# A long convolution's kernel spectrum: kept on chip in data rows, with only a parts-exchanged copy moved

## The chip, the cores and the metric

One core of a Trainium2 chip. The metric is the device time of one execution in microseconds (us). Single executions of the kernel before lie between 512.5 and 520.0 us; one of 522.9 us was slow and is not used. The profile is of one execution each.

## The reference, cut to what matters

Two layers of local attention and two layers of a long convolution alternate. Both convolutions use the same filter `K`, so its spectrum is made once, in the first convolution, and used in both.

```python
def _B_ref(u, ...):                                   # called twice
    K  = einsum("dn,dnl,dn->dl", Cc, P, dB).real      # same K in both calls
    Kf = rfft(pad(K));  Uf = rfft(pad(u))
    y  = irfft(Uf * Kf)[..., :L]                      # + u * Dskip
```

## The kernel before: the parts that matter

The FFT is done with matrices. Per convolution there are two groups of channels (g = 0, 1), and per group 8 chunks of the spectrum. `f1` is the first step of the forward transform (evacuated into `a1s`), `f2` the second, `i1` and `i2` are the inverse. A PSUM tile is named `pb`; `evac` copies it out with ScalarE (ACT) or VectorE (DVE).

```python
def k_f2(self, g):                     # spectrum of the filter, first convolution only
    def consume(p2, ec):
        kf = self.wk.tile([P, DQG, EC], BF16, name="kf_sb")       # pool of 3
        self.evac(kf[:], p2[:]...)
        self.nc.sync.dma_start(self.kf_dram[g, ec]..., kf[:]...)  # 256 KB to HBM

def u_f2(self, g):                     # spectrum of u, and the products
    ...                                # kf_ring: 4 slots (8 in the second convolution)
    def consume(p2, ec):
        kc = ring[:, slot]
        for h in range(2):             # 2 x 256 KB from HBM
            nc.sync.dma_start(ring[h::2, slot], self.kf_dram[g, ec])
        ub = self.wk.tile([P, DQG, EC], BF16, name="ub")
        nc.scalar.copy(ub[:], p2[:]...)
        nc.vector.tensor_tensor(t1[...], ub[:], kc[:, 0], ALU.mult)
        nc.vector.tensor_tensor(t2[...], ub[:], kc[:, 1], ALU.mult)

def i1(self, g):
    z = self.z0 if g == 0 else ...     # z0 is the buffer xnT
    for t in range(NQT):
        p3 = self.ptile(...)
        for j in range(DQT):
            nc.tensor.matmul(p3[:, j], lhsT=t1[:, dql], rhs=wp_r,  start=True,  stop=False)
            nc.tensor.matmul(p3[:, j], lhsT=t2[:, dql], rhs=wpj_r, start=False, stop=True)
        self.evac(z[...], p3[...])     # with pattern act, act, act, dve: tiles 3 and 7 on VectorE

# main program, first convolution
zip_run(fb.f1(0, kp, "ka"))
zip_run(fb.f1(1, kp, "ka"), fb.k_f2(0), lead=2)
zip_run(fb.f1(0, u, "ua"), fb.k_f2(1), lead=2)
fb.pat = ("act", "act", "act", "dve")
zip_run(fb.f1(1, u, "ua"), fb.u_f2(0), lead=2)
zip_run(fb.u_f2(1), fb.i1(0), lead=4)          # products of group 1 beside inverse of group 0
fb.pat = ("act", "dve")
zip_run(fb.i1(1), fb.i2(0, None), lead=2)      # needs all products of group 1
```

Outside of sections marked with `manual_schedule`, the order of the instructions on each engine is chosen when the kernel is built, not by the order of these lines.

Of the kernel before, what the change touches and what calls it, by code (L numbers as in the profile page):

```python
# [11 lines left out]
ALU = mybir.AluOpType  # L12
# [3 lines left out]
BF16 = mybir.dt.bfloat16  # L16
# [3 lines left out]
P = 128  # L20
S = 2048
D = 512
# [3 lines left out]
NA = 16  # L26
NDT = 4
# [8 lines left out]
DQG = 64  # L36
EC = 16
NEC = 128 // EC
# [84 lines left out]
class LayerA:  # L123
# [88 lines left out]
            self.kT[:, ft, e0:e1, 1:P], self.kT[:, ft, e0 + 16:e1 + 16, 0:P - 1])  # L212

    def load_wv(self, pool):
        self.wv = pool.tile([P, NDT, D], BF16, name="wv")
        self.nc.sync.dma_start(self.wv[:], self.wsrc[:, :, 2 * D:3 * D])

    def load_wo(self, pool):
# [239 lines left out]
            u_apply(14, range(14, 16))  # L458

    def load_w2(self, w2_dram):  # L460
        w2 = self.keep.tile([P, P * P], BF16, name="w2_sb", tag="slot")
        self.w2 = w2[:].rearrange("p (e c) -> p e c", c=P)
        for c in range(4):
            self.nc.sync.dma_start(self.w2[:, c * 32:(c + 1) * 32, :], w2_dram[:, c * 32:(c + 1) * 32, :])

    def close_logits(self):
        self.lctx.close()
# [13 lines left out]
def build_b_consts(nc, cpool, tmp, w2_dram):  # L481
# [29 lines left out]
    def off_cols(name, rcol, v00, v10, v01, v11):  # L511
        o = tmp.tile([P, 2], F32, name=name)
        nc.vector.tensor_scalar(o[:, 0:1], rcol, float(v10 - v00), float(v00), ALU.mult, ALU.add)
        nc.vector.tensor_scalar(o[:, 1:2], rcol, float(v11 - v01), float(v01), ALU.mult, ALU.add)
        return o
# [2 lines left out]
    eo = tmp.tile([P, 1], F32, name="w2_eo")  # L518
    nc.vector.scalar_tensor_tensor(eo[:], ak, 64.0, d4k, ALU.mult, ALU.mult)
    nc.vector.tensor_tensor(off[:], off[:], eo[:].to_broadcast([P, 2]), ALU.add)  # L520
    wps = (("Wp", (4, 8, 0, 4)), ("WpJ", (8, 12, 4, 8)))
    wo = {name: off_cols("off_" + name, rim, *offs) for name, offs in wps}
    zt = tmp.tile([P, 1024], BF16, name="w2_zero")
    nc.gpsimd.memset(zt[:], 0.0)
# [82 lines left out]
class FftB:  # L607
# [58 lines left out]
            yield  # L666

    def k_f2(self, g):
        def consume(p2, ec):
            kf = self.wk.tile([P, DQG, EC], BF16, name="kf_sb")  # L670
            self.evac(kf[:], p2[:].rearrange("p e q -> p q e"))
            self.nc.sync.dma_start(self.kf_dram[g, ec].rearrange("p r q e -> (p r) (q e)"), kf[:].rearrange("p q e -> p (q e)"))
        yield from self.f2(g, "ka", consume)

    def u_f2(self, g):
        nc = self.nc
        if self.kf_ring is None:
            self.kf_ring = [self.ring_pool.tile([P, 4, 2, DQG, EC], BF16, name="kf_ring", tag="kp")]
            if self.ring2 is not None:
                self.kf_ring.append(self.ring2.tile([P, 4, 2, DQG, EC], BF16, name="kf_ring2"))  # L680
        t1 = self.gtile("t1", [P, DQG, P])
        t2 = self.gtile("t2", [P, DQG, P])
        self.S[g]["t"] = (t1, t2)

        def consume(p2, ec):
            ring, slot = self.kf_ring[self.nkf // 4 % len(self.kf_ring)], self.nkf % 4
            kc = ring[:, slot]
            self.nkf += 1
            for h in range(2):
                nc.sync.dma_start(ring[h::2, slot], self.kf_dram[g, ec])  # L690
            ub = self.wk.tile([P, DQG, EC], BF16, name="ub")
            nc.scalar.copy(ub[:], p2[:].rearrange("p e q -> p q e"))  # L692
            nc.vector.tensor_tensor(t1[:, :, ec * EC:(ec + 1) * EC], ub[:], kc[:, 0], ALU.mult)  # L693
            nc.vector.tensor_tensor(t2[:, :, ec * EC:(ec + 1) * EC], ub[:], kc[:, 1], ALU.mult)  # L694
        yield from self.f2(g, "ua", consume)

    def i1(self, g):
# [353 lines left out]
def kernel(  # L1051
# [16 lines left out]
    nc = tc.nc  # L1068
# [19 lines left out]
    la = LayerA(tc, nc, consts, lnst, A_wqkv, A_wo, 0, xnT, 2)  # L1088

    C = {}  # L1090
    with tc.manual_schedule(engines={ET.DVE, ET.Activation, ET.PE, ET.SP}):
        k_gen(tc, nc, consts["ident"], ins, kd, la, x_v, lnst, lambda sp: build_b_consts(nc, cpool, sp, w2_dram), C)
# [4 lines left out]
    kpp = krctx.enter_context(tc.tile_pool(name="kp", bufs=1))  # L1097
    kp = kpp.tile([P, P, NA, 4], BF16, name="k_perm", tag="kp")
# [38 lines left out]

    z0 = xnT[:].rearrange("p t c -> p (t c)").rearrange("p (m c) -> p m c", m=2 * NA)
    fb = FftB(tc, nc, C, consts["ident"], w2_dram, g2_dram, kf_dram, x_sb, 0)
    fb.z0, fb.ring_pool, fb.w2 = z0, kpp, la.w2  # L1140
    fb.open_mid()
    zip_run(fb.f1(0, kp, "ka"))
    zip_run(fb.f1(1, kp, "ka"), fb.k_f2(0), lead=2)
# [7 lines left out]
    la = LayerA(tc, nc, consts, lnst, A_wqkv, A_wo, 1, xnT, 1)  # L1151
# [19 lines left out]
    fb = FftB(tc, nc, C, consts["ident"], w2_dram, g2_dram, kf_dram, x_sb, 1)  # L1171
# [54 lines left out]
```

## Time and profile before

I cut the first convolution into three stages by VectorE's timeline: **K** from its first evacuation of `a1s` to the first product, **U** from the first to the last product, **I** from the end of the last product to the start of its last evacuation of `z`.

| kernel before | from, us | length, us | VectorE busy, us | TensorE clock |
|---|---|---|---|---|
| K: spectrum of the filter | 231.06 | 30.56 | 24.50 | 1.00 |
| U: spectrum of u, products, first inverse half | 261.62 | 31.79 | 23.53 | 0.93 |
| I: second inverse half | 293.41 | 14.98 | 6.12 | 0.82 |
| whole kernel | 0 | 511.9 | 414.7 | 0.94 |

These are lines of the windows view of the kernel before (from:to, length, then busy time and count of PE, PEld, DVE, ACT, POOL, then granted clock, DMA share, GB/s):

```profile
261.62:293.41 31.79, 20.21 (x406) 18.12 (x404) 23.53 (x36) 22.73 (x24) 0.35 (x1) 0.93 0.76 249
293.41:308.39 14.98, 14.94 (x173) 14.03 (x172) 6.12 (x5) 5.95 (x6) 0.00 (x0) 0.82 0.00 1
```

Stage I is TensorE's: busy 14.94 of 14.98 us. In U no engine is full. VectorE's timeline of the kernel before (start, length, instruction; in brackets the idle time before it and what ended it):

```profile
271.39 0.69 DVE L693 TENSOR_TENSOR t<-ub,kf_ring 128x1024 bf16<-128x1024 bf16 x1 [0.58 <-DMA kf_ring<-kf_dram]
...
275.10 0.69 DVE L693 TENSOR_TENSOR t<-ub,kf_ring 128x1024 bf16<-128x1024 bf16 x1 [0.70 <-DMA kf_ring<-kf_dram]
...
283.91 1.22 DVE L644 CAST xnT<-pb 128x1024 bf16<-128x1024 f32 x1 [4.93 <-PE pb L709]
...
288.58 1.22 DVE L644 CAST xnT<-pb 128x1024 bf16<-128x1024 f32 x1 [1.04 <-PE pb L709]
```

The short waits are for the ring, the long one is for an inverse tile: an `xnT` evacuation stands in VectorE's order before products that could have run.

### The profile page before, as it was taken

The page shows a single profiled execution, that of the slowest core. Times are in us where ns is not written, and L with a number is a line of the kernel's source. Part 1 is how long each engine was busy: PE and PEld are TensorE (multiplying, and loading weights), DVE is VectorE, ACT ScalarE, POOL GpSimd, SP SyncE. Part 2 cuts the span into 40 slices and gives each one's busy share as a digit, 9 for nine tenths or more (in the row PEclk, how much of TensorE's full clock was granted, in tenths as well). Part 3 has the DMA queues.
Part 4 walks back from the last instruction along what each step waited for, and adds up shares of the span by engine and source line. Part 5 has one row for each costly group of instructions (what it writes and reads, how often), then busy time and mean ns, then how long its engine had stood idle before and what let it go on. Part 6 is the DMA issues. An engine that isn't in the chain of part 4 may idle for free.

```text
span 511.9 us, 12810 instructions
## 1 busy us (share of the span) xinstructions
PE 379.2 (74%) x5528; PEld 283.9 (55%) x5528; DVE 414.7 (81%) x580; ACT 336.5 (66%) x538; POOL 35.1 (7%) x38
## 2 busy tenths in 40 slices
PE   1000428898998998888876596889998898877795
PEld 1000216665655776667765495445657676676694
DVE  7799979999899999959776647728999999659843
ACT  5999597755554688588696534574543466679832
POOL 2000120000000011210000000100000022200000
PEclk9999978999998799899998989799997899979989
DMA  8803500111128338221788502540041061206314
GB/s 223 341 1 38 85 0 3 42 24 45 19 71 261 109 97 333 72 83 71 257 264 305 181 1 70 178 164 2 2 122 25 1 272 58 79 7 193 139 44 123
DMA packets 56122, 56.40 MB, mean 110 GB/s; under 512 B 28573, under 2 KB 45570, under 8 KB 54786
## 3 DMA queue, kind: packets, MB, share of 16 engines
q1 hardware_dynamic: 55922, 55.46, 34.8%
q8 instruction: 43, 0.70, 0.6%
q10 hardware_dynamic: 144, 0.13, 0.2%
q14 instruction: 13, 0.11, 0.1%
HBM read 38.67 MB, written 13.24 MB: 101 GB/s over the span
## 4 chain that ended last, share of the span: by engine, by line
PE 41%; DVE 23%; ACT 20%; DMA 6%; issue 4%; SPq 2%; POOL 2%; DVEq 0%; POOLq 0%; ACTq 0%
DVE pav L343 6%; PE pp L202 6%; PE pq L296 5%; PE po L351 4%; PE pq L143 4%; PE pk L975 3%; PE L L254 3%; DVE prod L247 3%; PE pb L708 3%; PE pb L709 2%; ACT ub L692 2%; DMA kf_dram<-kf_sb 2%; POOL ln_rstd L101 2%; ACT xnT L195 2%; PE pq L363 2%
## 5 line engine op out<-in xcount | busy, mean ns | idle before, releaser
L351 PE MATMUL po<-ident,pav 128*128 128x128 bf16 x1024 | 68.3, 229 | 14.4 <-DVE pav L343 14.4
L351 PEld LDWEIGHTS <-pav 128*128 128x128 bf16 x1024 | 63.8, 103 | 22.8 <-DVE pav L343 19.2
L343 DVE TENSOR_TENSOR pav<-attn,v_ext 128x4096 bf16<-128x4096 bf16 x32 | 72.9, 2283 | 0.8 <-PE po L351 0.8
L247 DVE TENSOR_TENSOR prod<-qT,kT_ext 128x4096 bf16<-128x4096 bf16 x29 | 65.8, 2285 | 3.2 <-PE L L254 3.1
L101 POOL TENSOR_TENSOR ln_rstd<-ln_rstd,ln_mh 128x4 f32<-128x4 f32 (+1 forms) x18 | 29.4, 1634 | 291.2 <-DVE ln_rstd L100 245.2
L708 PE MATMUL pb<-Wp,t 128*128 128x128 bf16 x256 | 36.0, 237 | 12.1 <-DVE t L693 7.4
L202 PE MATMUL pp<-xnT,kT_ext 128*128 128x512 bf16 x128 | 34.4, 416 | 7.2 <-ACT xnT L195 6.9
L644 ACT CAST a1s<-pb 128x1024 bf16<-128x1024 f32 x34 | 34.1, 1029 | 7.7 <-PE pb L655 6.8
L354 ACT CAST oT<-po 128x512 bf16<-128x512 f32 x32 | 18.5, 579 | 30.9 <-PE po L351 30.9
L193 PE MATMUL pt<-ident,x_blk 128*128 128x128 bf16 x64 | 5.6, 241 | 41.5 <-ACT x_blk L118 41.5
L709 PE MATMUL pb<-WpJ,t 128*128 128x128 bf16 x256 | 35.2, 237 | 0.4 <-DVE t L694 0.4
L664 PE MATMUL pb<-a1s,w_sb 128*128 128x64 bf16 x768 | 29.6, 194 | 7.9 <-ACT ub L692 4.2
L363 PE MATMUL pq<-wop,oT 128*128 128x512 bf16 x128 | 34.9, 397 | 0.0
L975 PE MATMUL pk<-B_t,A_t 128*64 128x84 bf16 (+1 forms) x512 | 25.3, 210 | 12.3 <-issue 9.3
L692 ACT CAST ub<-pb 128x1024 bf16<-128x1024 f32 x32 | 32.1, 1058 | 2.9 <-DVE t L694 2.9
L664 PEld LDWEIGHTS <-w_sb 128*128 128x128 bf16 x768 | 26.6, 98 | 11.2 <-issue 8.8
L708 PEld LDWEIGHTS <-t 128*128 128x128 bf16 x256 | 27.1, 107 | 9.4 <-DVE t L693 9.3
L298 ACT CAST v_ext<-pq 128x512 bf16<-128x512 f32 x32 | 18.8, 586 | 20.4 <-PE pq L296 20.4
L254 PEld LDWEIGHTS <-prod 128*128 128x128 bf16 x928 | 27.4, 96 | 8.0 <-DVE prod L247 1.6
L975 PEld LDWEIGHTS <-A_t 128*64 128x64 bf16 (+1 forms) x512 | 23.1, 110 | 15.6 <-issue 12.4
L296 PE MATMUL pq<-wv,xnT 128*128 128x512 bf16 x128 | 30.4, 379 | 0.0
L143 PE MATMUL pq<-xnT,kT_ext 128*128 128x512 bf16 x128 | 30.4, 380 | 0.0
(204 smaller groups left out, 883.3 us busy)
## 6 DMA issues: line engine op xcount, KB each, us to landing
kf_ring<-kf_dram SPq DMA_DIRECT2D x64, 256.0 KB
w_sb<-w_dram SPq DMA_DIRECT2D x8, 1024.0 KB
w_dram<-w_zero SPq DMA_DIRECT2D x1, 4096.0 KB
kf_dram<-kf_sb SPq DMA_DIRECT2D x16, 256.0 KB
v_ext<-v_ext SPq DMA_DIRECT2D x4, 784.0 KB
x_blk<-in_A_x_dram SPq DMA_DIRECT2D x4, 512.0 KB
kT_ext<-in_A_wqkv_dram SPq DMA_DIRECT2D x4, 512.0 KB
x_sb<-in_A_x_dram SPq DMA_DIRECT2D x4, 512.0 KB
```

Source lines behind the costliest of these rows:

```text
L143: nc.tensor.matmul(pq[:], lhsT=self.wqk[:, dt, ft * P:(ft + 1) * P], rhs=self.xnT[:, dt, q * 512:(q + 1) * 512], start=(dt == 0), stop=(dt ...
L202: nc.tensor.matmul(pp[:], lhsT=self.wqk[:, dt, D + ft * P: D + (ft + 1) * P], rhs=self.xnT[:, dt, b * 512:(b + 1) * 512], start=(dt == 0), ...
L247: nc.vector.tensor_tensor(pr, self.qT[q][:, ft].unsqueeze(1).to_broadcast([P, W, 4, P]), kap, ALU.mult)
L254: self.nc.tensor.matmul(L[:, al, w, ft * 8:(ft + 1) * 8], lhsT=pr[:, w, al, :], rhs=self.c["ind8"][:], start=False, stop=True, skip_group_ ...
L296: nc.tensor.matmul(pp[:], lhsT=xnT[:, dt, a * P:(a + 1) * P], rhs=wv[:, dt, :], start=(dt == 0), stop=(dt == NDT - 1))
L343: nc.vector.tensor_tensor(pv[:], attn[:, n % 4].unsqueeze(2).to_broadcast([P, W, DH, H]), vap, ALU.mult)
L351: nc.tensor.matmul(po[:, ft, :], lhsT=pvf[:, w, ft * P:(ft + 1) * P], rhs=ident[:], start=(w == 0 and ft == 0), stop=(w == W - 1), skip_gr ...
L363: nc.tensor.matmul(pw[:], lhsT=oT[:, ftp, :], rhs=wo[:, ftp, :], start=False, stop=(ftp == NDT - 1))
L664: nc.tensor.matmul(p2[:, j, :], lhsT=self.w2[:, ec * EC + j, :], rhs=a1s[:, ec * EC + j, :], start=True, stop=True)
L708: nc.tensor.matmul(p3[:, j, :], lhsT=t1[:, dql, :], rhs=wp_r, start=True, stop=False)
L709: nc.tensor.matmul(p3[:, j, :], lhsT=t2[:, dql, :], rhs=wpj_r, start=False, stop=True)
L975: nc.tensor.matmul(o, lhsT=lhs, rhs=Bt[:, ri, c * CH + ql].rearrange("p b g -> p (b g)"), start=(not half and j % 4 == 0 and ri == 0), sto ...
```

## The change

The intent: in the first convolution the filter spectrum need not go to HBM and back. Its 16 chunks get 16 places of their own in SBUF, whose old contents are dead by then, and `t1 = U*K` reads them in place. Only the copy with exchanged real and imaginary rows, for `t2`, is moved, from SBUF to SBUF. Since the rows of `t1` and `t2` now stand for other parts, the inverse tables get other offsets. The store to HBM stays, for the second convolution, which reloads in three transfers a chunk instead of two.

```diff
     def load_wv(self, pool):
-        self.wv = pool.tile([P, NDT, D], BF16, name="wv")
+        self.wv_pool = pool
+        self.wv = pool.tile([P, NDT, D], BF16, name="wv", tag="wv")
 ...
+    def spare(self):
+        rest = [self.w2_rest] + [self.keep.tile([P, 2 * DQG * EC], BF16, name=f"kn_{i}", tag="qT", bufs=2)[:] for i in range(2)]
+        rest.append(self.wv_pool.tile([P, 2 * DQG * EC], BF16, name="kn_2", tag="wv")[:])
+        ...                                      # cut into 9 places
 ...
-    wps = (("Wp", (4, 8, 0, 4)), ("WpJ", (8, 12, 4, 8)))
+    wps = (("Wp", (4, 12, 0, 8)), ("WpJ", (8, 8, 4, 4)))
 ...
     def k_f2(self, g):
+        if g == 0:
+            self.nat = list(self.spare)
+        else:
+            kp2 = self.ring_pool.tile([P, 8, DQG, EC], BF16, name="kf_nat", tag="kp")
+            self.kf_ring = kp2
+            self.nat += [kp2[:, 4 + i] for i in range(4)]
         def consume(p2, ec):
-            kf = self.wk.tile([P, DQG, EC], BF16, name="kf_sb")
-            self.evac(kf[:], p2[:].rearrange("p e q -> p q e"))
+            n = g * NEC + ec
+            if n >= len(self.nat):
+                self.nat.append(self.wk.tile([P, DQG, EC], BF16, name="kf_sb")[:])
+            kf = self.nat[n]
+            self.evac(kf, p2[:].rearrange("p e q -> p q e"))
             ...                                  # store to kf_dram as before
+    def kf_pair(self, g, ec):
+        n, sync = self.nkf, self.nc.sync
+        self.nkf += 1
+        if self.tag == 0:
+            kn, ks = self.nat[n], self.kf_ring[:, n % 4]
+            for h in range(2):
+                sync.dma_start(ks[h::2], kn[1 - h::2])        # 2 x 128 KB inside SBUF
+            return kn, ks
+        ...                                      # second convolution
+        sync.dma_start(kc[0::2], self.kf_dram[g, ec])
+        for r in range(2):
+            sync.dma_start(kc[1::2, r], self.kf_dram[g, ec, :, 1 - r])
+        return kc[:, 0], kc[:, 1]
 ...
-            nc.vector.tensor_tensor(t1[...], ub[:], kc[:, 0], ALU.mult)
-            nc.vector.tensor_tensor(t2[...], ub[:], kc[:, 1], ALU.mult)
+            nc.vector.tensor_tensor(t1[...], ub[:], kn, ALU.mult)
+            nc.vector.tensor_tensor(t2[...], ub[:], ks, ALU.mult)
```

More of the change, by code (lines that the diff above doesn't have):

```diff
@@ L460, in load_w2 @@
     def load_w2(self, w2_dram):
-        w2 = self.keep.tile([P, P * P], BF16, name="w2_sb", tag="slot")
-        self.w2 = w2[:].rearrange("p (e c) -> p e c", c=P)
+        w2 = self.keep.tile([P, NDT * (2 * D + (NA + 14) * P)], BF16, name="w2_sb", tag="slot")
+        self.w2 = w2[:, 0:P * P].rearrange("p (e c) -> p e c", c=P)
+        self.w2_rest = w2[:, P * P:]
         for c in range(4):
             self.nc.sync.dma_start(self.w2[:, c * 32:(c + 1) * 32, :], w2_dram[:, c * 32:(c + 1) * 32, :])
+    def spare(self):
+        rest = [self.w2_rest] + [self.keep.tile([P, 2 * DQG * EC], BF16, name=f"kn_{i}", tag="qT", bufs=2)[:] for i in range(2)]
+        rest.append(self.wv_pool.tile([P, 2 * DQG * EC], BF16, name="kn_2", tag="wv")[:])
+        n = DQG * EC
+        return [r[:, i * n:(i + 1) * n].rearrange("p (q e) -> p q e", e=EC) for r in rest for i in range(r.shape[-1] // n)]
     def close_logits(self):
@@ L668, in k_f2 @@
     def k_f2(self, g):
-        def consume(p2, ec):
-            kf = self.wk.tile([P, DQG, EC], BF16, name="kf_sb")
-            self.evac(kf[:], p2[:].rearrange("p e q -> p q e"))
-            self.nc.sync.dma_start(self.kf_dram[g, ec].rearrange("p r q e -> (p r) (q e)"), kf[:].rearrange("p q e -> p (q e)"))
-        yield from self.f2(g, "ka", consume)
+        if g == 0:
[4 more added lines that the diff above has]
+            self.nat += [kp2[:, 4 + i] for i in range(4)]
+        def consume(p2, ec):
+            n = g * NEC + ec
[3 more added lines that the diff above has]
+            self.evac(kf, p2[:].rearrange("p e q -> p q e"))
+            self.nc.sync.dma_start(self.kf_dram[g, ec].rearrange("p r q e -> (p r) (q e)"), kf.rearrange("p q e -> p (q e)"))
+        yield from self.f2(g, "ka", consume)
+    def kf_pair(self, g, ec):
[6 more added lines that the diff above has]
+            return kn, ks
+        if self.kf_ring is None:
+            self.kf_ring = [pool.tile([P, 4, 2, DQG, EC], BF16, name=f"kf_ring{i}")
+                            for i, pool in enumerate((self.ring_pool, self.ring2))]
+        kc = self.kf_ring[n // 4 % 2][:, n % 4]
+        sync.dma_start(kc[0::2], self.kf_dram[g, ec])
+        for r in range(2):
+            sync.dma_start(kc[1::2, r], self.kf_dram[g, ec, :, 1 - r])
+        return kc[:, 0], kc[:, 1]
     def u_f2(self, g):
         nc = self.nc
-        if self.kf_ring is None:
-            self.kf_ring = [self.ring_pool.tile([P, 4, 2, DQG, EC], BF16, name="kf_ring", tag="kp")]
-            if self.ring2 is not None:
-                self.kf_ring.append(self.ring2.tile([P, 4, 2, DQG, EC], BF16, name="kf_ring2"))
         t1 = self.gtile("t1", [P, DQG, P])
@@ L685, in consume @@
         def consume(p2, ec):
-            ring, slot = self.kf_ring[self.nkf // 4 % len(self.kf_ring)], self.nkf % 4
-            kc = ring[:, slot]
-            self.nkf += 1
-            for h in range(2):
-                nc.sync.dma_start(ring[h::2, slot], self.kf_dram[g, ec])
+            kn, ks = self.kf_pair(g, ec)
             ub = self.wk.tile([P, DQG, EC], BF16, name="ub")
             nc.scalar.copy(ub[:], p2[:].rearrange("p e q -> p q e"))
-            nc.vector.tensor_tensor(t1[:, :, ec * EC:(ec + 1) * EC], ub[:], kc[:, 0], ALU.mult)
-            nc.vector.tensor_tensor(t2[:, :, ec * EC:(ec + 1) * EC], ub[:], kc[:, 1], ALU.mult)
+            nc.vector.tensor_tensor(t1[:, :, ec * EC:(ec + 1) * EC], ub[:], kn, ALU.mult)
+            nc.vector.tensor_tensor(t2[:, :, ec * EC:(ec + 1) * EC], ub[:], ks, ALU.mult)
         yield from self.f2(g, "ua", consume)
@@ L1139 @@
     fb = FftB(tc, nc, C, consts["ident"], w2_dram, g2_dram, kf_dram, x_sb, 0)
-    fb.z0, fb.ring_pool, fb.w2 = z0, kpp, la.w2
+    fb.z0, fb.ring_pool, fb.w2, fb.spare = z0, kpp, la.w2, la.spare()
     fb.open_mid()
```

## The prediction

> **What bounds the kernel now.** I read the page first, then the chain of waits and VectorE's timeline in the stretch that the diff touches, then the windows view. The whole-kernel shares do not decide anything: no engine is full, and the chain passes from one to the other.
>
> ```profile
> PE 379.2 (74%) x5528; PEld 283.9 (55%) x5528; DVE 414.7 (81%) x580; ACT 336.5 (66%) x538; POOL 35.1 (7%) x38
> ...
> PE 41%; DVE 23%; ACT 20%; DMA 6%; issue 4%; SPq 2%; POOL 2%; DVEq 0%; POOLq 0%; ACTq 0%
> ```
>
> The reader should see that transfers hold only 6% of the chain, some 30 us; a change of transfers can win a part of that and no more. Which part is in the chain by time:
>
> ```profile
> 237.10 1.14 DVE kf_sb L644
> 238.26 2.43 DMA kf_dram<-kf_sb
> ...
> 243.19 3.94 DMA kf_dram<-kf_sb
> ...
> 248.48 3.49 DMA kf_dram<-kf_sb
> ...
> 253.34 2.41 DMA kf_dram<-kf_sb
> ...
> 268.94 4.05 DMA kf_ring<-kf_dram
> ```
>
> Four stores of the kernel spectrum and one reload, 16.3 us, lie on the chain. The reason is buffers: the spectrum leaves PSUM into a pool of three (kf_sb), so evacuation n waits until store n-3 has landed. VectorE's timeline shows it (in brackets: idle before, and its releaser):
>
> ```profile
> 240.81 3.49 DVE L644 CAST kf_sb<-pb 128x1024 bf16<-128x1024 f32 x3 [0.32 <-DMA kf_dram<-kf_sb]
> 245.03 1.23 DVE L644 CAST a1s<-pb 128x1024 bf16<-128x1024 f32 x1 [0.73 <-PE pb L655]
> 247.23 3.48 DVE L644 CAST kf_sb<-pb 128x1024 bf16<-128x1024 f32 x3 [0.98 <-DMA kf_dram<-kf_sb]
> 252.09 3.49 DVE L644 CAST kf_sb<-pb 128x1024 bf16<-128x1024 f32 x3 [1.38 <-PE pb L664]
> 255.88 1.22 DVE L644 CAST kf_sb<-pb 128x1024 bf16<-128x1024 f32 x1 [0.30 <-DMA kf_dram<-kf_sb]
> 259.20 1.23 DVE L644 CAST kf_sb<-pb 128x1024 bf16<-128x1024 f32 x1 [2.10 <-DMA kf_dram<-kf_sb]
> ```
>
> Groups of three evacuations and then a pause: the signature of a pool of three. The windows view (length, busy time of each engine, clock, DMA share, GB/s) gives the two stages, and the same second stage in the second convolution:
>
> ```profile
> 231.00:260.60 29.60, 23.48 (x661) 21.21 (x661) 23.54 (x22) 22.77 (x25) 0.00 (x0) 1.00 0.56 188
> 260.60:293.50 32.90, 21.32 (x437) 19.03 (x435) 24.55 (x36) 23.75 (x26) 0.35 (x1) 0.93 0.76 250
> 461.00:487.30 26.30, 18.65 (x413) 16.87 (x407) 23.34 (x36) 22.93 (x25) 0.00 (x0) 0.99 0.49 162
> ```
>
> In the first line VectorE is busy 23.5 of 29.6 us. The second line (first convolution, products of spectra) and the third (second convolution) hold the same 32 products, but the first one takes 6.6 us more, with DMA engines at 0.76 against 0.49. The third line needs no reload for the first half: the ring was filled long before. So it is a picture of the stage without transfers in its way.
>
> [...] the stores here took 2.41 to 3.94 us[...] windows of 2 us after the stall of 270 to 273.7 show a clock of 0.76 and 0.50. [...] the products here take 0.60 us for 1024 elements start to start against 1.16 us for an evacuation[...].
>
> **The change, part by part.**
>
> (1) First convolution, making the spectrum. The 16 chunks get 16 places of their own (3 in the rest of the weight slot, 4 in two q tiles, 2 in the wv tile, 4 in the ring, 3 kf_sb). The compiled order shows the evacuations waiting on TensorE alone; the 16 stores stay, for the second convolution, but nobody waits for them. Before: from 231.06 to 260.48, 29.4 us, VectorE does 5 + 14 + 1 = 20 evacuations of 1.16 us (3.48 for three) = 23.2 us; 6.0 us are idle: 3.7 put down to stores, 2.3 to TensorE. The last is partly an echo: ScalarE, too, waited 1.75 us for a store at 244.6, which held a PSUM buffer. TensorE comes close behind, one pair of tiles each 1.14 us (236.58 to 237.72 to 238.86), so I leave 1.0 us of bubbles: 24.3 us. Gain 5.1 us.
>
> (2) First convolution, products. Before: per chunk two transfers of 256 KB from HBM, 16 x 0.52 = 8.4 MB, after a store landed. Now: one copy with exchanged parts, two transfers of 128 KB inside SBUF, 4.2 MB; t1 reads the spectrum in place. The ring of swapped copies still has four slots. At the pace of the second convolution (a chunk each 1.2 us), from the second product of chunk n-4 to that of chunk n there are 1.2 x 4 - 0.6 = 4.2 us. The copy needs two issues at about 0.5 us (median 0.587 for the old ones)[...] VectorE idled 0.58, 0.42 and 0.70 us. VectorE from first to last product: before 261.62 to 293.41 = 31.8 us; second convolution 461.50 to 487.27 = 25.8 us. The 6.0 us between split into about 2 us of waits on the ring and about 4 us in which VectorE waited for TensorE (4.93 and 1.04 against 2.11), partly at half clock after the stall. I count 4.9 us, leaving 1.1 for copies that come late and for the other order of the inverse tiles.
>
> (3) Second convolution: reload in three transfers instead of two per chunk, same 8.4 MB, 16 more issues at 0.6 us = 9.6 us of the queue. The first eight chunks are loaded in the attention before. For the last eight, 3 x 0.6 = 1.8 us a chunk from 462.8 on: chunk 8 is there at about 467, needed at 473.0; chunk 15 at about 480, needed at 486.0. Cost 0.
>
> (4) The inverse tables: other numbers in the same instructions, cost 0. The count of matmuls and products stays.
>
> Sum: 5.1 + 4.9 = 10.0 us, all in front of the rest of the kernel, so it passes to the end: 516.4 - 10.0 = 506.4 us, a ratio of 0.981.
>
> **Rivals.**
> A. The stage of products keeps its length. The swapped copies are still a chain of release, issue, landing and product over four slots; if landing takes 4 us under the remaining stores[...], the chain is 0.1 + 1.0 + 4.0 + 0.6 = 5.7 us for four chunks, 1.4 instead of 1.2 each, and the scheduler puts more products ahead of the inverse evacuations (14 chunks before the first one, where it was 11), so a wait there holds TensorE too. [...] Against it: half the bytes. Then only (1) and some 2 us stay: 509.5 us.
> B. TensorE becomes the bound. With no stalls it runs at 1.14 us a pair against VectorE's 1.16; a clock below 1 there would give back 1 to 3 us. Against it: it had 1.00 all through that stage. About 508.5 us.
> C. More than the stalls goes away: without idle gaps the clock stays up in the inverse transform too (it was 0.58 from 293.5 to 300, 0.75 in the same place of the second convolution). Another 2 us: 504 us.
> D. The evacuation was hidden and only the order changes: 515 us. The idle times on the chain speak against it.
>
> **Range and chances.** The sum and rivals span 504 to 509.5; repeated runs of the kernel before spread from 514.65 to 519.14, which adds some 2 us. Range 502 to 512. The 2% line is at 506.0, just under my number: rival C and the full 6.0 us of part 2 lie beyond it, A and B on this side. Faster 0.47, same 0.52, slower 0.01.
>
> **What would show it.** Step 1 right: no evacuation of the spectrum waits for a store, and the 20 evacuations span about 24.3 us. Step 2 right: products from first to last in about 27 us, waits for the swapped copies under 1 us in sum; wrong (rival A) if VectorE waits for them again and again. Step 3 right: the second convolution's products still take about 25.8 us with no wait on the ring. Rival B: a clock under 1 in the first stage. Rival C: the inverse transform after the last product shorter than its 18 us. The prediction fails upwards if part 2 gains nothing, downwards if the clock gains as well.

## The result, and the profile after

| | median, us | range, us | ratio to before, 95% interval |
|---|---|---|---|
| before, 4 runs | 515.55 | 514.65 to 519.14 | |
| changed, 4 runs | 499.58 | 497.57 to 500.10 | 0.9671 [0.9615, 0.9726] |
| changed, second time, 6 runs (before: 516.28) | 501.20 | 500.61 to 502.02 | 0.9717 [0.9679, 0.9756] |

All outputs are right. Executions over 1.5% slower than the fastest of the same kernel are left out of the means. Here and below a ratio is the mean time of one kernel's runs over that of the other's of the same rounds, so it is not quite the ratio of the medians beside it. The change is faster by some 3%, and the number predicted, 506.4 us, was too high by 6.8 us; the measured median lies 2.4 us under the range (0.8 us under it the second time).

The same three stages, from the profiled executions:

| stage | before, us | after, us | gain, us | predicted gain, us |
|---|---|---|---|---|
| K | 30.56 | 25.82 | 4.74 | 5.1 |
| U | 31.79 | 24.15 | 7.64 | 4.9 |
| I | 14.98 | 11.94 | 3.04 | 0 |
| start of K | 231.06 | 231.65 | -0.59 | 0 |
| after the last `z` of I to the end | 203.51 | 204.74 | -1.23 | 0 |
| span | 511.9 | 498.3 | 13.6 | 10.0 |

(The profiled execution of before was a quick one, 513.64 us, and that of after the slowest of its four; so the two spans differ by 13.6 us where the medians differ by 16.0.)

The windows view of the changed kernel, same cuts:

```profile
257.47:281.62 24.15, 18.73 (x408) 17.02 (x407) 23.11 (x35) 22.43 (x24) 0.35 (x1) 1.00 0.53 181
281.62:293.56 11.94, 11.90 (x170) 11.19 (x168) 6.12 (x6) 5.95 (x6) 0.00 (x0) 1.00 0.01 4
```

VectorE does the same 23 us of work in U, now in 24.15 us instead of 31.79: of 8.26 us of idle time 1.04 are left. Stage I holds the same work for TensorE, at a clock of 1.00 instead of 0.82. VectorE's timeline of the changed kernel answers to the groups of three evacuations that the prediction shows, and to the waits above:

```profile
237.60 3.47 DVE L653 CAST w_sb<-pb 128x1024 bf16<-128x1024 f32 x3
241.00 4.60 DVE L653 CAST kn<-pb 128x1024 bf16<-128x1024 f32 x4
...
247.78 4.60 DVE L653 CAST kf_nat<-pb 128x1024 bf16<-128x1024 f32 x4
...
276.86 1.21 DVE L653 CAST xnT<-pb 128x1024 bf16<-128x1024 f32 x1
...
279.80 1.23 DVE L653 CAST xnT<-pb 128x1024 bf16<-128x1024 f32 x1
```

No bracket on any of them: no evacuation of the spectrum waits for a store, and no inverse tile is waited for. The experiments below show that transfers alone do not explain the second. Counting VectorE's multiplications around the two `xnT` evacuations gives **22, 4 and 6 in the kernel before, 28, 3 and 1 in the changed one**. The diff doesn't order this: the build chose another order. In the chain of waits of the changed kernel transfers have gone from 6% to 2%:

```profile
PE 42%; DVE 25%; ACT 21%; issue 5%; DMA 2%; SPq 2%; POOL 2%; POOLq 0%; DVEq 0%; ACTq 0%
```

Why is stage I shorter? In the kernel before the last six multiplications come after the second `xnT` evacuation, and TensorE has nothing to do meanwhile. Its timeline, and the clock in windows of 2 us (third number from the end of a line):

```profile
292.86 0.50 PE L708 MATMUL pb<-Wp,t 128*128 128x128 bf16 x3 [4.32 <-DVE t L693]
...
293.76 0.31 PE L708 MATMUL pb<-Wp,t 128*128 128x128 bf16 x1
293.87 0.31 PE L709 MATMUL pb<-WpJ,t 128*128 128x128 bf16 x1
```

```profile
289.00:291.00 2.00, 0.00 (x0) 0.00 (x0) 2.00 (x4) 1.18 (x2) 0.00 (x0) 1.00 0.96 305
...
293.00:295.00 2.00, 2.00 (x19) 1.74 (x18) 0.41 (x1) 0.00 (x0) 0.00 (x0) 0.50 0.01 4
...
297.00:299.00 2.00, 2.00 (x18) 1.81 (x17) 1.11 (x1) 0.52 (x1) 0.00 (x0) 0.51 0.00 0
```

After 4.32 us without work the clock is at 0.50, and matmuls start each 0.11 us (293.55 to 298.13) instead of each 0.055 us (before the wait, 286.0 to 286.9). The clock is back at 1.00 at 298.96, 6.1 us after the first of them. In the changed kernel only one multiplication is left there, and TensorE's waits at that place are 0.69 and 0.30 us:

```profile
280.56 0.22 PE L737 MATMUL pb<-Wp,t 128*128 128x128 bf16 x1 [0.69 <-ACT xnT L653]
...
281.08 0.27 PE L751 MATMUL pb<-x_sb,ident 128*128 128x256 bf16 x1 [0.30 <-DVE xnT L653]
```

So the theory after the result: (a) the evacuation gains what was worked out; (b) in U the change acts twice, by fewer bytes to wait for and by the order of VectorE's instructions, which also takes away the 4.32 us of idle time, after which the clock in I was at 0.50. A rival for (b): the order is beside the point, and the gain in U is that of the transfers' source (SBUF instead of HBM) or size. The experiments take these apart.

### The profile page after: what moved, and what is told of

The parts are those of the page before. It is cut to its first block, busy times and chain, and to the rows that moved or that the text cites.

```text
span 498.3 us, 12784 instructions
## 1 busy us (share of the span) xinstructions
PE 372.0 (75%) x5492; PEld 280.7 (56%) x5528; DVE 414.1 (83%) x580; ACT 336.0 (67%) x538; POOL 34.9 (7%) x38
## 4 chain that ended last, share of the span: by engine, by line
PE 42%; DVE 25%; ACT 21%; issue 5%; DMA 2%; SPq 2%; POOL 2%; POOLq 0%; DVEq 0%; ACTq 0%
DVE pav L344 7%; PE pp L202 6%; PE po L352 5%; PE pq L297 4%; PE pq L143 4%; PE pk L1004 3%; DVE prod L248 3%; PE L L255 3%; ACT ub L721 3%; PE pb L664 3%; PE pb L738 2%; ACT xnT L195 2%; PE pb L737 2%; ACT a1s L653 2%; PE pq L364 2%
## 5 line engine op out<-in xcount | busy, mean ns | idle before, releaser
L202 PE MATMUL pp<-xnT,kT_ext 128*128 128x512 bf16 x123 | 33.1, 408 | 7.6 <-ACT xnT L195 6.9
L737 PE MATMUL pb<-Wp,t 128*128 128x128 bf16 x256 | 32.5, 224 | 7.0 <-DVE t L722 3.1
L364 PE MATMUL pq<-wop,oT 128*128 128x512 bf16 x112 | 31.4, 395 | 1.4 <-ACT oT L355 0.4
L738 PE MATMUL pb<-WpJ,t 128*128 128x128 bf16 x256 | 32.0, 225 | 0.0
L205 ACT CAST kT_ext<-pp 128x512 bf16<-128x512 f32 x32 | 18.4, 586 | 15.2 <-PE pp L202 15.2
```

The lines of the kernel that those rows point to most:

```text
L202: nc.tensor.matmul(pp[:], lhsT=self.wqk[:, dt, D + ft * P: D + (ft + 1) * P], rhs=self.xnT[:, dt, b * 512:(b + 1) * 512], start=(dt == 0), ...
L737: nc.tensor.matmul(p3[:, j, :], lhsT=t1[:, dql, :], rhs=wp_r, start=True, stop=False)
```

## The experiments

**One part alone: places for the spectrum.** The kernel before, with the evacuation spread over nine places used in turn; reload and order as before.

```diff
-            kf = self.wk.tile([P, DQG, EC], BF16, name="kf_sb")
+            kf = self.spare[(g * NEC + ec) % len(self.spare)]
```

> Part 1 alone: the kernel before, with nine places of their own for the evacuated spectrum in turn (so evacuation n waits for store n-9, not n-3), and the full reload of 512 KB a chunk kept. VectorE's compiled order is that of the kernel before. Theory (the two parts add): from VectorE's first evacuation to the first product 25.8 us instead of 30.6, the products from first to last still about 31.8 us, the clock still near 0.5 in the inverse transform after them; 5 us won, about 510.5 us. Rival (the transfers only pile up behind the faster evacuations, and the reloads now wait for the stores): the products stretch by 2 to 4 us, and only 1 to 3 us are won, 512.5 to 514.5 us.

Measured: 510.49 us, ratio 0.9902 [0.9864, 0.9939], that is 5.1 us (1 - 0.9902 of some 515.8). K is 27.05 us; U gets no shorter, 33.35 us. VectorE's timeline in U, of this kernel:

```profile
269.93 0.69 DVE L702 TENSOR_TENSOR t<-ub,kf_ring 128x1024 bf16<-128x1024 bf16 x1 [1.32 <-DMA kf_ring<-kf_dram]
...
282.57 1.23 DVE L653 CAST xnT<-pb 128x1024 bf16<-128x1024 f32 x1 [4.58 <-PE pb L718]
```

Part 1 holds, in size too. The ring's waits and the long wait for the inverse tile are all still there, so nothing of the gain in U comes from part 1. (In the profiled run K is 3.51 us shorter, I is 1.01 shorter and U 1.56 longer, 2.96 us in all; the ratio's interval stands for 3.1 to 7.0 us, so that 5.1 meets the forecast to a tenth is luck.) K comes in two lengths, 25.8 and 27.0 us, also in later kernels that do not differ from each other there, and the clock tells them apart: in the four runs with 27.0 us TensorE ran at half clock for 3.41 us near the start of K, in those with 25.8 us nowhere in K. This run had the longer one (windows view):

```profile
234.03:237.44 3.41, 3.41 (x72) 3.41 (x68) 2.45 (x2) 2.43 (x3) 0.00 (x0) 0.50 0.02 5
```

**Where the swapped copy comes from.** The changed kernel, but each copy is read from the stored spectrum in HBM; same size, same number.

```diff
-                sync.dma_start(ks[h::2], kn[1 - h::2])
+                sync.dma_start(ks[h::2], self.kf_dram[g, ec, :, 1 - h])
```

> The changed kernel, but the copy with exchanged parts is taken from the stored spectrum in HBM instead of from SBUF: same 128 KB per transfer, same 4.2 MB, same compiled order of VectorE; only the source and the wait for the store differ. If the gain is from half the bytes and from the spectrum being used in place, the time stays at 499.6 us within 1.5 us. If it matters that the copy does not go through HBM, each copy lands later, the products wait for it (0.5 us or more a chunk) and the time is 502 to 506 us.

Measured: 500.12 us, ratio 0.9706 [0.9676, 0.9736]; K 25.83, U 24.15, I 11.95 us, the same as the changed kernel to 0.01 us. That the copy stays on chip is not what pays; the source is out as a cause. What is left is the halved size (4.2 MB instead of 8.4), `t1` that waits for no transfer, and the order.

**VectorE in program order.** The kernel before, with VectorE's order in U fixed to that of the program's lines.

```diff
+    with tc.manual_schedule(engines={ET.DVE}):
+        zip_run(fb.f1(1, u, "ua"), fb.u_f2(0), lead=2)
+        zip_run(fb.u_f2(1), fb.i1(0), lead=4)
```

> The kernel before with one thing changed: VectorE runs the stage of products in program order, so all 16 chunks come before the two evacuations of the first inverse stage (in the kernel before they stand after chunk 11 and chunk 13). Buffers and transfers are those of before. Theory (the order leaves TensorE idle before the second inverse stage, the idle time halves its clock): the idle gap before that stage shrinks from 4 us to 2 or less, the clock stays at 1.00, the inverse stage is some 3 us shorter and the products end some 3 to 5 us sooner: 507 to 510 us. Rival (only the transfers count): reloads hold the products as before, nothing is won: 514 to 516 us.

Measured: 512.54 us, ratio 0.9949 [0.9904, 0.9994]; K 34.78, U 28.91, I 14.06 us. The edit also moved the evacuations of `a1s` and delayed the first product, so that K grew by 4.2 us while U shrank by 2.9, and the split between stages is not that of the other kernels. The forecast that the clock would stay up failed: it was at half for 3.41 us at the start of I, and I got only 0.9 us shorter; in K, too, lie 8.8 us at half clock, which the profile of the kernel before does not show there. The run is inconclusive: the two halves of the order were changed together. The later pair of experiments fixes the order only in the second half of U.

**The clock alone.** The kernel before, with 64 matmuls of the identity by itself put before the second inverse half, where TensorE waits for the last products. Their result is overwritten.

```diff
             p3 = self.ptile([P, DQT, P])
+            if t == 0 and (self.tag, g) in self.warm:          # (0, 1): 64
+                for _ in range(self.warm[self.tag, g]):
+                    nc.tensor.matmul(p3[:, 0, :], lhsT=self.ident[:], rhs=self.ident[:], start=True, stop=True)
```

> The kernel before with 64 matmuls of the identity, whose result is overwritten, put on TensorE just ahead of the second inverse stage, where it is idle for 4 us; nothing else moves. If the half clock of 293 to 299 us follows from that idle time and costs the 3 us by which the changed kernel's inverse transform is shorter, then the clock stays at 1.00 there, the time from the last product to the last z evacuation falls from 15.0 to about 12.0 us, and the whole takes about 512.5 us. If the clock is halved for another reason, or the inverse transform is short for its order, the time stays at 515.5 us or grows by up to 1 us.

Measured: 513.12 us, ratio 0.9954 [0.9926, 0.9981]; U 31.48 us (as before), I 12.38 instead of 14.98 us. The filler's last part and the first matmuls of I in TensorE's timeline, and a window of 2 us with its clock, of this kernel:

```profile
293.79 1.22 PE L709 MATMUL pb<-ident 128*128 128x128 bf16 x19
295.75 0.34 PE L712 MATMUL pb<-Wp,t 128*128 128x128 bf16 x3 [0.73 <-DVE t L694]
```

```profile
297.00:299.00 2.00, 2.00 (x39) 1.99 (x37) 0.77 (x1) 1.01 (x1) 0.00 (x0) 1.00 0.04 8
```

The inverse half does 39 matmuls in a window of 2 us where it did 18. So the clock accounts for 2.60 of the 3.04 us by which I is shorter after the change, with nothing else altered in I or in the order (K was 1.46 us longer in this profiled run, with 3.41 us at half clock). The whole time follows with 2.4 us (1 - 0.9954 of 515.8).

**Bytes and order, each alone.** Two kernels complete a table of two by two. One is the changed kernel with VectorE's old order: 22, 4 and 6 multiplications around the `xnT` evacuations. The other is the kernel with places of its own (old reload of 2 x 256 KB), with the new order, in whole chunks: 28, 2 and 2.

```diff
+            def products(): ...                                 # the two multiplications
+            if self.tag == 0 and g == 1 and ec >= 3:            # >= 6 in the other kernel
+                self.later.append(products)
+            else:
+                products()
 ...
+            if self.tag == 0 and g == 0 and t in (3, 7):        # in i1, after an evacuation of VectorE
+                for _ in range(2 if t == 3 else 3):             # 1 and 1 in the other kernel
+                    self.later.pop(0)()
 ...
+    with tc.manual_schedule(engines={ET.DVE}):
+        zip_run(fb.u_f2(1), fb.i1(0), lead=4)
```

> The changed kernel, buffers and transfers untouched, but VectorE is made to take the order of the kernel before in the last eight chunks (first inverse evacuation after chunk 11, second after chunk 13, three chunks last). Theory A (the gain beyond my sum is the order: with it TensorE has work until the last products): VectorE waits 2 to 4 us for inverse tiles again, products from first to last 26 to 28 us instead of 24.2, TensorE idle for about 4 us before the second inverse stage, clock halved there, inverse stage 13.5 to 15 us instead of 11.9; total 503 to 506 us. Theory B (the gain is the halved transfers alone): products 24.2 us, inverse stage 11.9 us, total 499.6 us within 1.5.

> Run e1_places (own places, full reload of 512 KB a chunk) with VectorE put in the order of the changed kernel: 14 chunks, an inverse evacuation, a chunk, an evacuation, a chunk. Theory A (order alone): products fall from 33.4 us to about 26, inverse stage from 14.0 to 12, total 501 to 503 us. Theory B (transfers alone): products stay at 33, total 510.5 us. Theory C (both are needed: the reload at about 1.8 us a chunk still paces all chunks, but without the waits for inverse tiles and with a full clock after it): products about 30 us, inverse stage 12 us, total 504 to 507 us.

| us (ratio to before, interval) | old order | new order |
|---|---|---|
| reload 2 x 256 KB (own places) | 510.5 (0.9902 [0.9864, 0.9939]) | 507.1 (0.9846 [0.982, 0.9872]) |
| copy 2 x 128 KB (changed kernel) | 505.6 (0.9803 [0.9773, 0.9832]) | 499.6 (0.9671 [0.9615, 0.9726]) |

The order is worth 510.5 - 507.1 = 3.4 us with the old transfers and 505.6 - 499.6 = 6.0 us with the new ones. The new transfers are worth 4.9 us in the old order and 7.5 us in the new one. Neither is the whole. Together they give 10.9 us where the two parts alone give 3.4 + 4.9 = 8.3, but that they more than add is not shown: U and I of the four profiled executions give 11.2 against 10.5 us, and single executions of one of these kernels lie up to 4 us apart. The old order with the new transfers came out where its theory A said; the new order with the old transfers 0.1 us above theory C's range, and "order alone" and "transfers alone" both missed. Both forced orders use a manual schedule of VectorE; it goes with a loss in one kernel and a gain in the other, so it is not the schedule as such. The old order with the new transfers brings the old picture back (VectorE's timeline of that kernel, and its clock):

```profile
277.11 1.22 DVE L654 CAST xnT<-pb 128x1024 bf16<-128x1024 f32 x1 [3.31 <-PE pb L744]
```

```profile
283.00:285.00 2.00, 0.00 (x0) 0.00 (x0) 2.00 (x4) 0.23 (x1) 0.00 (x0) 1.00 0.08 25
285.00:287.00 2.00, 1.08 (x9) 0.83 (x10) 1.46 (x3) 0.00 (x0) 0.00 (x0) 0.55 0.00 0
```

U is 27.89 us, I is 13.36 us. TensorE is idle from about 282 to 286 and the clock falls (0.55 from 285 to 287), as in the kernel before. With the new order and the old transfers U is 30.50 us and I 12.38: VectorE still waits for the ring, up to 1.36 us at a time, and the clock is down at another place, 0.50 from 269 to 275. (This profile is of the quickest of its five executions, 504.2 us; the others lie from 507.1 to 507.9.)

```profile
275.44 0.69 DVE L704 TENSOR_TENSOR t<-ub,kf_ring 128x1024 bf16<-128x1024 bf16 x1 [1.33 <-DMA kf_ring<-kf_dram]
```

**Better than both: the second convolution.** The changed kernel's second convolution has an order of 26, 2 and 4 multiplications (24, 4 and 4 before the change), an idle time of TensorE of 3.12 us before its second inverse half, and a lowered clock (0.72 in the four us around the end of that wait, 0.55 in the first 4.5 us after the first `a1s` evacuation). Two places of filler: before its second inverse half and before its first transform.

```diff
+        self.warm    = {(1, 1): 64}           # before i1 of group 1
+        self.warm_f1 = {(1, 0, "ua"): 64}     # before f1 of group 0
```

> The changed kernel with 64 idle matmuls of the identity at two places of the second convolution: ahead of its first transform, where TensorE had nothing to do for 5.5 us, and ahead of its second inverse stage. If the half clock follows from idle time there as it did in the first convolution: clock 1.00 in both places, 2 to 3 us won in the transform and 1.5 in the inverse stage, total 495 to 496.5 us. If those stages are not bound by TensorE: 499.6 us or up to 1 us more.

Measured: 497.97 us, ratio 0.9658 [0.9632, 0.9684]. In the second convolution the time from the first `a1s` evacuation to the first product fell from 8.94 to 7.37 us and I from 13.84 to 12.33 us, with a clock of 1.00 throughout, as the theory said; the time missed its 495 to 496.5 us. From the first product of the first convolution to the end the profiled runs took 240.83 us (changed) and 236.99 us (this one), 3.84 us less; the medians differ by only 1.6 us, and the intervals of the two ratios overlap. A part of the reason is in the run with the swapped copy from HBM: it has no filler and the same wait, yet its clock stayed up. TensorE's timeline and then the windows view just after the wait, of the changed kernel:

```profile
473.23 0.34 PE L737 MATMUL pb<-Wp,t 128*128 128x128 bf16 x3 [3.12 <-DVE t L722]
```

```profile
471.98:475.98 4.00, 2.71 (x26) 2.43 (x27) 1.79 (x3) 0.33 (x1) 0.00 (x0) 0.72 0.02 4
```

And the same two views of the kernel with the copy from HBM:

```profile
473.61 0.34 PE L737 MATMUL pb<-Wp,t 128*128 128x128 bf16 x3 [3.12 <-DVE t L722]
```

```profile
472.36:476.36 4.00, 2.70 (x44) 2.43 (x45) 2.06 (x4) 1.01 (x1) 0.00 (x0) 1.00 0.02 4
```

The same idle time of 3.12 us was followed by 0.72 in one run and by 1.00 in the other. The traces show where the two differ. The trace of a profiled execution holds the stretches of the granted clock with their lengths. In those of the kernel before and of the changed kernel every change of the clock lies on a grid of 3.41 us, and a stretch at half clock lasts 3.41, 6.83 or 10.24 us (but for the last one, which runs to the end). The grid does not lie at the same place in two executions: its edges around the wait are at 470.33 and 473.74 us in the changed kernel (wait until 473.23) and at 468.75, 472.16 and 475.57 us in the kernel with the copy from HBM (wait until 473.61). The windows view cut at the grid of the changed kernel, and then at that of the kernel with the copy from HBM, with the same wait inside:

```profile
470.33:473.74 3.41, 0.51 (x5) 0.28 (x5) 3.41 (x5) 0.53 (x1) 0.00 (x0) 1.00 0.00 0
473.74:477.15 3.41, 3.37 (x33) 3.32 (x33) 0.03 (x1) 1.01 (x1) 0.00 (x0) 0.50 0.02 5
```

```profile
468.75:472.16 3.41, 1.74 (x32) 1.57 (x29) 2.19 (x3) 2.50 (x3) 0.00 (x0) 1.00 0.02 7
472.16:475.57 3.41, 1.91 (x30) 1.64 (x30) 2.00 (x4) 0.30 (x1) 0.00 (x0) 1.00 0.02 5
```

In the changed kernel nearly the whole wait lay in one step, which held 0.51 us of matmuls (TensorE's busy time), and the next step ran at half clock. In the other kernel the wait was split over two steps, which held 1.74 and 1.91 us of matmuls, and the clock stayed up. So the filler can only save the clock where it would have fallen. The kernel with the copy from HBM had its second convolution in 7.48, 25.80 and 12.27 us with no filler at all, as quick as the filler's; whether this is the whole gap between 3.84 and 1.6 us stays open, as each kernel has only one profiled execution.

**The changed kernel again, and the order forced on the second convolution too.** The same chip for both.

```diff
+            if self.tag == 1 and g == 1 and ec >= 6:            # as above, second convolution, one and one
+                self.later.append(products)
```

> The changed kernel once more, five rounds, beside the next run on the same chip. Expected 499.6 us and a ratio of 0.967 to the kernel before, as the first time; the interval narrower than 0.9615 to 0.9726. First convolution as before: products 24.2 us, inverse stage 11.9 us; second convolution: from the first evacuation of a1s to the first product 8.9, products 25.8, inverse stage 13.8 us.

> The kernel with filler matmuls of the second convolution, plus VectorE's order of the first convolution forced on the second one: 14 chunks of products, inverse tile, one chunk, inverse tile, one chunk (it was 13, 1, 2). Theory (the order of VectorE sets the length of the products stage): VectorE's waits of 0.90 and 1.22 us for inverse tiles shrink, products from 25.8 to about 24.2 us, the filler's 12.3 us of inverse stage stay: 496.4 us, some 3 us under the changed kernel. Rival (the second convolution is bound by other things, ScalarE's 8.0 of 8 us from 446 to 470, so order is worth nothing there): products stay at 25.8 and the time at 498 us, as the kernel with filler matmuls alone had.

The changed kernel: 501.20 us, stages as the first time to within 0.02 us. The kernel with the order: 496.13 us, ratio 0.9625 [0.9582, 0.9667]. That looks like the theory's number, but the profile says otherwise. Products fell from 25.80 to 24.62 us, and I rose from 12.33 to 13.55 us: the sum is 38.17 us where it was 38.13. The filler was in the way (TensorE's timeline of this kernel):

```profile
466.60 3.73 PE L748 MATMUL pb<-ident 128*128 128x128 bf16 x64
```

The last product had ended at 469.21, and the inverse matmuls stood behind the filler until 470.17. The median's gain over the kernel with the filler alone must come from elsewhere (the two were also taken on different chips and in different rounds): from the first convolution's first product to the second's first `a1s` evacuation this profiled run took 179.22 us against 180.88, with a clock that was mostly higher (0.98 against 0.88 in one stretch of 10 us, 1.00 against 0.87 in another), which the edit does not touch on purpose. Where the grid of 3.41 us lay in either execution is a candidate; it was not tested.

**A filler that fits, and none.** 40 matmuls instead of 64, and none before the inverse half (the filler before the first transform stays).

```diff
-        self.warm = {(1, 1): 64}
+        self.warm = {(1, 1): 40}              # the other kernel: {}
```

> The kernel of both fillers and the order of 14, 1, 1 chunks, with 40 filler matmuls instead of 64 before the second inverse stage of the second convolution. There the 64 took 3.73 us and ended at 470.17, though the last product had ended at 469.21, and products plus inverse stage came to 38.17 us, as without the new order (38.13). Theory (the filler itself ate the order's gain by standing 1.0 us in front of the inverse matmuls): 40 take 2.3 us and end before the last product; inverse stage from 13.6 to 12.4 us, sum 37.1, time 495.1 us. Rival (the second convolution's end is bound by ScalarE or by the inverse tiles, whatever the filler): sum stays at 38.2 us, 496.1 us.

> The same with no filler before the second inverse stage (the filler before the first transform stays). TensorE then has nothing from 466.6 to 469.2, 2.6 us, where the changed kernel had 3.1. Theory ([...] the order alone, which shortens the idle time, is enough): clock 1.00 in the inverse stage, which takes 12.4 us as with 40 fillers, 495.1 us. Rival (any idle time beside the thinly filled stretch before it lets the clock fall): clock 0.7 to 0.85 in the first 8 us after the products, inverse stage 13.9 us, 496.6 us.

| second convolution, us | products | I | sum | median of the kernel | ratio |
|---|---|---|---|---|---|
| changed kernel | 25.80 | 13.83 | 39.63 | 501.20 | 0.9717 |
| filler of 64, old order | 25.80 | 12.33 | 38.13 | 497.97 | 0.9658 |
| filler of 64, new order | 24.62 | 13.55 | 38.17 | 496.13 | 0.9625 |
| filler of 40, new order | 24.62 | 12.21 | 36.83 | 495.74 | 0.9601 |
| no filler, new order | 24.62 | 13.68 | 38.30 | 498.14 | 0.9642 |

The rows come from chips 3, 7, 3, 0 and 0; only those of one chip were run in the same rounds. The filler of 40 took 2.39 us and ended at 469.13, before the last product, and the clock was 1.00 after it, up to the end of I; the order's gain of 1.2 us then stays. So the theory held for the first kernel, with a sum of 36.83 us where it said 37.1, and fell for the second: without the filler TensorE's wait was shorter than in the changed kernel (1.92 us against 3.12), and the clock fell all the same (0.54). The step of 3.41 us before the fall held 1.49 us of matmuls, not none. How little work in a step goes before a fall is not settled by these runs. The clock fell after steps with 0.51 us (changed kernel) and 1.49 us; in the kernel before it fell at 275.04, after a step with 1.43 us, and at 292.14, after a step with none; in the kernel with own places and the new order it fell between 267 and 269, where the windows of 2 us from 265 to 269 hold 0.75 and 1.21 us. It did not fall after the steps with 1.74 and 1.91 us of the kernel with the copy from HBM. TensorE's timeline and a window of the kernel without the filler:

```profile
472.02 0.48 PE L751 MATMUL pb<-Wp,t 128*128 128x128 bf16 x3 [1.92 <-DVE t L729]
```

```profile
471.95:473.95 2.00, 1.93 (x17) 1.75 (x18) 0.62 (x2) 0.00 (x0) 0.00 (x0) 0.54 0.00 0
```

The kernel with the filler of 40 is by its median the fastest. Its interval [0.956, 0.9642] lies under that of the changed kernel's second measurement, [0.9679, 0.9756], and overlaps that of its first, [0.9615, 0.9726]; they were taken in different rounds (the second measurement on another chip). By the profiles it saves 2.8 us from the second convolution's first product to the end (47.48 us against 50.25); against the filler of 64 its gain (495.74 to 496.13) is within what single runs spread.

## Why the prediction was right or wrong

**Part 1, the evacuation: right.** 20 evacuations were to take 24.3 us; from the first to the next `a1s` after them they took 255.94 - 231.65 = 24.29 us, a gain of 5.13 us where 5.1 was said, and the kernel with this part alone gained 5.1 us by its ratio (interval 3.1 to 7.0). No evacuation waited for a store.

**Part 2, the products: the step that failed.** It reads: "I count 4.9 us, leaving 1.1 for copies that come late and for the other order of the inverse tiles." The gain was 7.64 us. Two things in it were wrong.
- The 1.1 us were set aside as a cost. There was none: no product waited for a copy (how soon a copy lands was my estimate, not shown by the trace of the kernel before), and the other order was a gain. The prediction had the order in hand, "14 chunks before the first one, where it was 11", and read it in rival A as a danger ("a wait there holds TensorE too"). The table of two by two shows it is worth 3.4 to 6.0 us of the whole time, by the medians.
- The second convolution, 25.8 us, was taken as the stage without transfers in its way and hence as the floor. It is not one: in the kernel before, VectorE waits 2.11 us for an inverse tile there, in the order 24, 4, 4 (in the changed kernel 0.90 and 1.22 us, in the order 26, 2, 4). Forcing the new order on it brought 24.62 us.

The lines of VectorE's timeline in the second convolution, of the kernel before and then of the changed one:

```profile
480.02 1.23 DVE L644 CAST xnT<-pb 128x1024 bf16<-128x1024 f32 x1 [2.11 <-PE pb L709]
```

```profile
466.50 1.22 DVE L653 CAST xnT<-pb 128x1024 bf16<-128x1024 f32 x1 [0.90 <-PE pb L738]
470.15 1.23 DVE L653 CAST xnT<-pb 128x1024 bf16<-128x1024 f32 x1 [1.22 <-PE pb L738]
```

The 1.1 us of reserve and the 25.8 - 24.15 = 1.65 us of false floor are the 2.74 us that the sum lacked in U. By the profiles U was 27.89 us with the new transfers in the old order, so the order makes 3.74 us of its gain.

**The tail: named, and not counted.** The sum has no term for stage I. Rival C said that the clock might stay up there and be worth 2 us; it was worth 2.6 us by the experiment with the filler, and stage I became 3.04 us shorter. What was missed is that rival C hangs on the order of part 2: the idle time of 4.32 us, after which the clock is at 0.50, is made by the six multiplications that follow the second inverse tile, visible in the profile of the kernel before. Had the order been read as a gain, C would have followed with it.

**Parts 3 and 4: right.** The second convolution's products took 25.79 us (before: 25.77) with no wait on the ring; the tables cost nothing that shows.

**Rivals.** A fell: no product waited for a swapped copy. B fell in the profiled execution: the clock was 1.00 in K, which took 25.82 us. But in four of the other profiled executions with these evacuations 3.41 us of K were at half clock and K took 1.2 us longer, so B's cost of 1 to 3 us is met in some of them. D fell with part 1. By the profiled spans the account closes: 10.0 predicted, - 0.36 in K, + 2.74 in U, + 3.04 in I, - 0.59 and - 1.23 outside the first convolution make 13.6 us. The last two are not explained; the starts of K in the eleven experiments range from 230.8 to 234.4 us, so the first of them is within what runs of these kernels differ by.

**What stays open.** Which of the build's inputs made it choose another order for VectorE was not tested: reading the copies from HBM kept the new order and moving only the places kept the old one, so it comes with the smaller transfers or with `t1` being free of them; no more can be said. That the new transfers (fewer bytes, `t1` in place) are worth 7.5 us in the new order and 4.9 in the old, by the medians, is measured, not taken apart further.

## What to carry to other kernels

Where a build orders instructions, compare the order before and after, and price it in both directions: an evacuation that stands before ready products is a wait in itself (4.93 us in the kernel before), and what stands last before the next stage decides how long the next engine idles (4.32 us with six multiplications last; with one, waits of 0.69 and 0.30 us). A stage that holds the same work elsewhere in the kernel is a floor only after its own waits have been subtracted (25.8 us here, with 2.11 us of wait for an inverse tile in it). And where a change removes an idle time of TensorE after which the trace shows a lowered clock, count the next stage at full clock too: here I went from 14.98 us at 0.82 to 11.94 us at 1.00 when the 4.32 us went. Where such an idle time stays, matmuls that end before the work arrives can fill it: with the new order in the second convolution 40 of them (2.39 us) brought products and I to 36.83 us, where it was 38.30 without filler, and 64 (3.73 us) gave the order's gain back (38.17).
